# A list scheduler in the host code orders the recurrence, the weight preparation and the early blocks

## The chip, the cores and the metric

One core of a Trainium2 chip runs the whole program. The metric is device time in microseconds (us), the median of three runs. PE is the matrix engine, DVE, ACT and POOL are the vector, scalar and general-purpose engines, SP issues nearly all DMAs. Every engine executes its own list of instructions strictly in order; between engines there are semaphores. So the order in which the host code writes instructions is the order in which each engine runs them.

## The reference

A linear recurrence over 768 steps (32 heads of width 40) feeds two MLP layers over 3072 tokens.

```python
for t in range(S):
    y[:, :, t] = einsum('bhd,bhde->bhe', rt, state)
    Sa = einsum('bhde,bhe->bhd', state, at)
    state = state * wt[:, :, None, :] - outer(Sa, bt) + outer(vt, kt)
x = y.transpose(0, 2, 1, 3).reshape(3072, 320)
x = square(relu(x @ w_in)) @ w_out          # layer 0, d_ff 2048
h = x @ w_in2
out = (h * cos(h)) @ w_out2                 # layer 1
```

## The kernel before

**Recurrence.** The 768 steps are cut into 12 chunks of 64. For each chunk: DVE makes running products of the decay (`decay`, tiles lam and il in cin), the inputs are scaled (`compact_kb` on DVE, `compact_a` on POOL), PE forms a gram matrix (`gt`, PSUM tile pgt, masked by DVE into ga), which goes through DRAM (`gt_out`, `solve_load`, tile Ls) to a triangular solve of 28 small steps (`solve`, on POOL, for chunk 0 on DVE; tiles lent or l and ttmp), back through DRAM (`solve_store`, `load_t`, tiles Ts and tcomp) to `join`, four products that complete the inverse (pn, pn, pw, pt; the first is evicted by DVE as l<-pn). Then four independent groups of heads run `state`: products pq, px, pu, py and pm, each evicted by ACT or DVE before the next; pm gives the state that the next chunk needs. `pmat` (pp) prepares a part from the inputs alone. From chunk 3 on the tile l holds both the solve's matrix and a factor of `join`, so a solve cannot begin before the join of the chunk before it is through.

**Weights.** Those of both layers arrive as 64-bit words; ACT, DVE (u<-u, u<-w) and POOL turn them into f32, and ACT and POOL split them into a high and a low part (ws). The first 8 of 16 tiles of layer 0 are prepared in the opening, the others and half of layer 1 later.

**MLP.** Six blocks of 512 tokens per layer, 16 slices f each. In layer 0 a slice is 8 matmuls into a PSUM bank h, then Relu, Square and a rounded copy on ACT (g, gh), the rest gl on POOL, and 8 matmuls into po. Layer 1 has 8 and 12 (h, pt). A block needs two chunks of the recurrence; the last block of layer 0 and all of layer 1 come after the recurrence. PSUM has 8 banks: until the recurrence ends 3 for po, 1 for h and 4 that its products share (pool att); then h gets a second bank.

**Order.** `opening()` interleaves chunks 0 to 2 with weights by hand (`weave`); `period(c)` has a table of 42 time slots for each later chunk, and MLP units are paid out evenly over them, so that a block is nearly done when the next becomes ready. Operations of DVE pass through a helper, so they all carry line 151; they are told apart by their tiles.

Of the kernel before, what the change touches and what calls it, by code (L numbers as in the profile page):

```python
# [134 lines left out]
class Vector:  # L135

    def __init__(self, nc):
        self.real = nc.vector  # L140
        self.chain, self.credit = None, 0

    def link(self):
        if self.chain is not None and next(self.chain, 0) == 0:
            self.chain = None

    def __getattr__(self, name):
        fn = getattr(self.real, name)

        def call(*args, **kwargs):  # L150
            fn(*args, **kwargs)  # L151
            if self.credit > 0:
                self.credit -= 1
                self.link()

        return call

    def finish(self):
        while self.credit > 0 and self.chain is not None:
            self.credit -= 1  # L160
            self.link()
# [160 lines left out]
class Attn:  # L322
# [316 lines left out]
    def state(self, c, g):  # L639

        nc = self.nc
        ga, rv, mov = self.ga[c, g // 2], self.rv.pop((c, g)), self.mov.pop((c, g))
# [66 lines left out]
class Mlp:  # L709


    def __init__(self, tc, ctx, i, kc, xs, x2s, out, vec):
        self.vec = vec
        self.tc, self.nc, self.i, self.kc = tc, tc.nc, i, kc
        self.xs, self.x2s, self.out = xs, x2s, out
        self.p1 = ctx.enter_context(tc.tile_pool(name="m1", bufs=1))
        self.p2 = ctx.enter_context(tc.tile_pool(name="m2", bufs=2))
        self.po = ctx.enter_context(tc.tile_pool(name="mpo", bufs=1, space=PSUM))
        self.ph = ctx.enter_context(tc.tile_pool(name="mph", bufs=1, space=PSUM))
        self.ws, self.raw, self.xf, self.done = {}, {}, {}, set()  # L720
        self.xn = None
        self.ph2 = self.p3 = self.w2 = self.pending = None
        self.whole, self.more = set(), None
# [255 lines left out]
SOLVE, END = 8, 19  # L979

JOIN, GIN = (27, 30, 33, 36, 36), (37, 38, 40, 41)

TURN = 5


class Program:
    def __init__(self, tc, ctx, i, out, nch):
# [11 lines left out]
        self.vec = Vector(tc.nc)  # L999
# [49 lines left out]
    def run(self):  # L1049
# [6 lines left out]
        self.w1, self.w2 = self.W.first(EARLY), chain(self.W.rest(EARLY), self.W.second())  # L1056
        self.M.more = self.w2
# [5 lines left out]
        self.ctx1.close()  # L1063
        self.M.p3 = self.ctx2.enter_context(self.tc.tile_pool(name="m3", bufs=1))
# [8 lines left out]
    @staticmethod  # L1073
    def weave(*lists):

        todo = [((k + 0.5) / len(z), j, k, fn) for j, z in enumerate(lists) for k, fn in enumerate(z)]
        for _, _, _, fn in sorted(todo, key=lambda z: z[:3]):
            fn()

    def opening(self):  # L1080

        A, M = self.A, self.M
        self.gts = {c: A.gt(c) for c in range(4)}
        self.dcs = {c: A.decay(c) for c in range(1, 5)}
        cks = {c: A.compact_kb(c) for c in range(4)}
        join = {c: A.join(c) for c in range(4)}
        st = {c: [A.state(c, g) for g in range(4)] for c in range(3)}

        def s(gen, n=1):
            return [lambda: step(gen)] * n  # L1090

        def f(fn, *args):
            return [lambda: fn(*args)]

        def w(n):
            return s(self.w1, n)

        def prepare(c):
            out = s(self.dcs[c], 6)
            for q in range(4):  # L1100
                out += s(self.dcs[c], 2) + s(cks[c])
                if q % 2:
                    out += f(A.compact_a, c, q // 2)
            return out

        def gram(c):
            out = []
            for h in range(2):
                out += s(self.gts[c], 6) + f(A.gt_out, c, h, 0) + f(A.gt_out, c, h, 1)
            return out + f(A.solve_load, c)  # L1110

        def load(c):
            return f(A.load_w, c) + f(A.load_kb, c) + f(A.load_a, c)

        def solve(c, eng, n=4):
            z = A.solve
            box = []

            def go():
                if not box:  # L1120
                    box.append(A.solve(c, eng))
                step(box[0], n)

            return [go] * -(-30 // n) + f(A.solve_store, c) + f(A.load_t, c)

        def gin(c):
            return [lambda h=h, par=par: A.gt_in(c, h, par) for h in range(2) for par in range(2)] if c else []

        def fetch(c, g):
            return f(A.rv_load, c, g) + f(A.mov_load, c, g) + f(A.pmat, c, g)  # L1130

        def states(c, h):
            a, b = st[c][2 * h:2 * h + 2]
            out = []
            for k in range(5):
                out += s(a) + s(b)
            return out + f(A.y_store, c, h)

        for z in load(1):
            z()  # L1140
        A.zero()
        dc, g0 = A.decay(0), self.gts[0]
        for j in range(4):
            for _ in range(3):
                next(dc)
            next(cks[0])
            if j == 0:
                A.identities()
            A.compact_a(0, j, 4)
            if j == 2:  # L1150
                step(g0, 3)
        d1 = prepare(1)
        step(g0, 3)
        A.gt_out(0, 0, 0)
        A.gt_out(0, 0, 1)
        for z in d1[:3]:
            z()
        step(g0, 3)
        for z in d1[3:4]:
            z()  # L1160
        step(g0, 3)
        A.gt_out(0, 1, 0)
        A.gt_out(0, 1, 1)
        A.solve_load(0)
        step(self.w1, 5)
        for z in d1[4:9]:
            z()
        A.rv_load(0, 0)
        A.rv_load(0, 1)
        self.weave(solve(0, self.vec.real, 3), d1[9:] + load(2), w(5))  # L1170
        self.weave(gram(1), w(4), fetch(0, 0)[1:] + fetch(0, 1)[1:])
        A.keep_a(0)
        A.keep_a(1)
        pool = solve(1, A.nc.gpsimd, 2)
        self.weave(s(join[0], 5), s(self.dcs[2], 6))
        d2 = prepare(2)[6:]
        self.weave(states(0, 0), fetch(0, 2) + fetch(0, 3), w(6), pool[:8], d2[:3])
        self.weave(states(0, 1), fetch(1, 0) + fetch(1, 1), w(6), pool[8:], d2[3:])
        self.weave(s(join[1], 5) + gin(1), gram(2))
        A.keep_a(0)  # L1180
        A.keep_a(1)
        pool = solve(2, A.nc.gpsimd, 2)
        d3 = prepare(3)
        self.weave(states(1, 0), fetch(1, 2) + fetch(1, 3), w(8), pool[:8])
        self.weave(states(1, 1), fetch(2, 0) + fetch(2, 1), w(8), pool[8:], load(3))
        while next(self.w1, 0) is None:
            pass
        M.load_x(0, 0)
        self.weave(s(join[2], 5) + gin(2), s(self.w2, 10), d3[:6])
        self.ready = 0  # L1190
        self.weave(d3[6:] + s(self.gts[3], 9) + f(A.gt_out, 3, 0, 0) + f(A.gt_out, 3, 0, 1) + f(A.load_w, 4)
                   + s(self.dcs[4], 6), s(self.w2, 32), f(self.mlp, 1) * 40)

    def period(self, c):

        A, nch = self.A, self.nch
        more = c + 1 < nch
        st = [A.state(c, g) for g in range(4)]
        todo, rate = {}, {}

        def at(t, f, *args):
            todo.setdefault(t, []).append((f, args))

        for half in range(2):
            for t in ((15, 19, 23, 27, 31) if c < 2 else (20, 24, 28, 32, 36)) if half else (0, 4, 10, 14, 18):
                for q in range(2):
                    at(t, step, st[2 * half + q])
        at(2, A.rv_load, c, 2)
        at(6, A.rv_load, c, 3)
        at(6, A.mov_load, c, 2)  # L1210
        at(9, A.pmat, c, 2)
        at(14 if c < 2 else 16, A.mov_load, c, 3)
        at(14 if c < 2 else 19, A.pmat, c, 3)
        at(19, A.y_store, c, 0)
        at(33 if c < 2 else 37, A.y_store, c, 1)
        if more:
            for t in (0, 1, 2):
                at(t, step, self.gts[c + 1])
            if c:
                at(3, A.gt_out, c + 1, 1, 0)  # L1220
                at(3, A.gt_out, c + 1, 1, 1)
            if c:
                at(6, A.solve_load, c + 1)
# [148 lines left out]
```

## Time and profile before

| | |
|---|---|
| median of 3 runs | 1293.3 us (1292.32 to 1296.19) |
| the profiled execution | 1293.86 us, span 1292.1 us |
| mean granted TensorE clock | 0.923 of full speed |
| busy share PE / DVE / ACT / POOL | 86% / 55% / 56% / 43% |

The time of an execution is its span and 1.8 us around it. Busy shares are means over three stages that differ: an opening without MLP, a stretch in which recurrence and MLP share PE, and a tail of MLP alone. A matmul's record lasts longer than the time it takes from the next one, so PE's pace is read from starts, not from durations.

### The profile page before, as it was taken

How to read it: one execution, taken by the hardware profiler on the slowest of the kernel's cores; microseconds unless marked ns; L12 is line 12 of the kernel's file. 1: busy time of each engine (PE TensorE's matmuls, PEld its weight loads, DVE VectorE, ACT ScalarE, POOL GpSimd, SP SyncE). 2: the span in 40 equal slices, each digit the busy share in tenths (PEclk: the TensorE clock that was granted, in tenths of full speed). 3: DMA queues.
4: the chain of work that ended last, by engine and by line, in shares of the span. 5: the costliest groups of instructions: out<-in, count | busy, mean ns of one | idle time of the engine just before them, and what ended most of it. 6: DMA issues, size and time to landing. Idle time of an engine off the chain costs nothing.

```text
span 1292.1 us, 32595 instructions
## 1 busy us (share of the span) xinstructions
PE 1116.6 (86%) x13314; PEld 922.8 (71%) x13314; DVE 707.6 (55%) x1327; ACT 718.8 (56%) x1460; POOL 550.1 (43%) x788
## 2 busy tenths in 40 slices
PE   2467558796778989999999999998999999999997
PEld 2456446575556767777777777777889999999996
DVE  6774757667556556665656544124497343444432
ACT  2244555454374747574747475647756565655554
POOL 3261725626434251625252523125787333333332
PEclk9985758878779898999999999998999999999999
DMA  7532712535364343634363432126301010101000
GB/s 183 140 99 39 187 53 74 103 82 110 89 143 104 90 95 82 143 81 95 80 141 70 93 86 64 33 59 207 100 24 40 7 46 1 45 1 46 1 21 24
DMA packets 205147, 102.73 MB, mean 80 GB/s; under 512 B 163052, under 2 KB 185580, under 8 KB 204156
## 3 DMA queue, kind: packets, MB, share of 16 engines
q1 hardware_dynamic: 203154, 99.85, 31.7%
q8 instruction: 107, 1.75, 0.6%
q10 hardware_dynamic: 1834, 0.70, 0.2%
q14 instruction: 52, 0.43, 0.1%
HBM read 77.43 MB, written 23.09 MB: 78 GB/s over the span
## 4 chain that ended last, share of the span: by engine, by line
PE 58%; ACT 10%; POOL 10%; issue 7%; DMA 7%; DVE 5%; SPq 2%; ACTq 0%; POOLq 0%; DVEq 0%
PE h L941 23%; PE pt L883 13%; PE po L893 9%; PE pgt L479 3%; DMA w<-moe 2%; POOL ttmp L526 2%; PE pu L669 2%; POOL gl L792 2%; POOL u L188 2%; POOL l L529 1%; DVE u L151 1%; PE py L679 1%; PE pn L572 1%; PE pn L567 1%; POOL ws L220 1%
## 5 line engine op out<-in xcount | busy, mean ns | idle before, releaser
L941 PE MATMUL h<-xh,ws 128*128 128x512 f32 x960 | 334.1, 410 | 28.1 <-ACT g L789 19.6
L792 POOL TENSOR_TENSOR gl<-g,gh 128x512 fp32r<-128x512 f32 x96 | 129.7, 1352 | 300.0 <-ACT gh L791 197.7
L941 PEld LDWEIGHTS h<-xh,ws 128*128 128x128 f32 x960 | 183.1, 193 | 76.2 <-ACT g L789 28.0
L941 PE MATMUL h<-xl,ws 128*128 128x512 f32 x576 | 234.6, 407 | 0.1
L820 POOL TENSOR_TENSOR gl<-g,gh 128x512 fp32r<-128x512 f32 x96 | 125.3, 1305 | 190.8 <-ACT gh L819 158.8
L893 PE MATMUL po<-gh,ws 128*128 128x512 f32 x480 | 148.0, 427 | 3.5 <-ACT o L839 3.5
L789 ACT ACTIVATE g<-h 128x512 f32<-128x512 f32 x96 | 56.8, 592 | 148.7 <-PE h L941 143.7
L883 PE MATMUL pt<-ws,gh 128*128 128x320 f32 x768 | 128.1, 308 | 0.5 <-DVE g L151 0.4
L941 PEld LDWEIGHTS h<-xl,ws 128*128 128x128 f32 x576 | 110.9, 193 | 23.3 <-issue 2.6
L883 PEld LDWEIGHTS pt<-ws,gh 128*128 128x128 f32 x768 | 119.9, 188 | 8.3 <-DVE g L151 0.6
L800 ACT ACTIVATE n<-h 128x512 int32<-128x512 f32 x96 | 57.3, 596 | 119.9 <-PE h L941 119.9
L151 DVE SCALAR_TENSOR_TENSOR g<-n,h 128x512 f32<-128x512 int32 x96 | 66.0, 688 | 103.6 <-ACT n L800 100.8
L479 PE MATMUL pgt<-at,cin 40*128 40x104 f32 x768 | 73.4, 336 | 50.0 <-POOL at L455 41.6
L893 PEld LDWEIGHTS po<-gh,ws 128*128 128x128 f32 x480 | 93.9, 201 | 28.1 <-ACT o L839 3.9
L151 DVE TENSOR_TENSOR g<-g,h 128x512 f32<-128x512 f32 x96 | 65.8, 686 | 71.7 <-ACT g L804 71.7
L479 PEld LDWEIGHTS pgt<-at,cin 40*128 40x128 f32 x768 | 63.1, 236 | 57.3 <-POOL at L455 44.2
L188 POOL TENSOR_TENSOR u<-u,w 128x256 int32<-128x256 int32 (+2 forms) x80 | 57.0, 712 | 99.8 <-DVE u L151 80.5
L151 DVE TENSOR_TENSOR ga<-pgt,kc 128x416 f32<-128x416 f32 x96 | 52.8, 584 | 73.2 <-PE pgt L479 72.9
L893 PE MATMUL po<-gl,ws 128*128 128x512 f32 x288 | 90.2, 411 | 0.0
L151 DVE TENSOR_SCALAR u<-u 128x160 f32<-128x160 f32 (+9 forms) x160 | 61.5, 384 | 42.7 <-ACT u L176 39.7
L804 ACT ACTIVATE g<-g,kc 128x512 f32<-128x512 f32 x96 | 69.7, 726 | 26.5 <-DVE g L151 25.0
L151 DVE TENSOR_TENSOR mov<-pu,kc 64x416 f32<-64x416 f32 x96 | 56.5, 589 | 43.3 <-PE pu L670 30.4
(121 smaller groups left out, 2332.5 us busy)
## 6 DMA issues: line engine op xcount, KB each, us to landing
rv<-rv SPq DMA_DIRECT2D x48, 256.0 KB
w<-moe SPq DMA_DIRECT2D x16, 704.0 KB
cin<-cin SPq DMA_DIRECT2D x8, 832.0 KB
Ls<-ga SPq DMA_DIRECT2D x48, 128.0 KB
w<-moe SPq DMA_DIRECT2D x32, 160.0 KB
w<-moe SPq DMA_DIRECT2D x16, 256.0 KB
mov<-vt SPq DMA_DIRECT2D x96, 40.0 KB
xs<-yt SPq DMA_DIRECT2D x48, 80.0 KB
```

Of the source, the lines that this page charges most:

```text
L151: fn(*args, **kwargs)
L188: self.nc.gpsimd.tensor_tensor(t.bitcast(I32), u.bitcast(I32), w[:, :, 0], op=ALU.add)
L479: nc.tensor.matmul(pv[par][:, j], self.kb[r0:r0 + 40, p0 + j].rearrange("p h b -> p (h b)"), self.at[r0:r0 + 40, p0 + j], start=True, stop ...
L526: eng.tensor_tensor(tv, L[:, 0:j, j:j + 1].to_broadcast([128, j, n]), L[:, j:j + 1, j + 1:16].to_broadcast([128, j, n]), op=ALU.mult)
L789: nc.scalar.activation(g, h, AF.Relu)
L792: self.later.append((2, lambda: nc.gpsimd.tensor_tensor(gl, g, gh, op=ALU.subtract)))
L800: nc.scalar.activation(n, h, AF.Copy, bias=0.25, scale=float(np.float32(1.0 / (2.0 * np.pi))))
L804: nc.scalar.activation(g, g, AF.Sin, bias=self.kc[:, K_QT:K_QT + 1])
L820: nc.gpsimd.tensor_tensor(gl, g, gh, op=ALU.subtract)
L883: nc.tensor.matmul(self.pos[j][:, 0:DM], x[:, 128 * j:128 * j + 128], wo[:, DM * ws:DM * ws + DM], start=(f == 0 and x is gh and ws == 0), ...
L893: nc.tensor.matmul(self.pos[m], wo[:, 128 * ws:128 * ws + 128], x, start=(f == 0 and k in (0, 2, 4)), stop=(f == NF - 1 and k in (5, 6, 7)))
L941: nc.tensor.matmul(h, wi[:, ws], x[:, kt], start=(k == 0), stop=(k == 7))
```

## The change

The host code no longer writes instructions as it comes to them. A recorder (`Book`, `Engine`, `View`) takes each call, notes which tile regions it reads and writes, prices it (`price`) and keeps it. `run()` calls all tasks of recurrence (kind c), weights (w) and blocks 0 to 4 of layer 0 (m) in a plain order; `flush()` then simulates the five engines and the DMAs and emits one operation after another: always on the engine that can begin earliest, the candidate that can start first there (`slack` is 0), and among those that tie by `key`. On PE an MLP operation comes behind every recurrence operation, and two matmuls of the MLP stay together; elsewhere MLP operations come first. The rank is the longest priced path to the end. When the last recurrence operation is placed, what is left of weights and MLP follows in program order. The operations themselves, their number and their engines stay as they are. In PSUM, att goes from 4 banks to 3, and the freed bank becomes a second h (`ph3`), used by odd slices until the recurrence ends.

```diff
-        att = self.ctx1.enter_context(tc.tile_pool(name="att", bufs=4, space=PSUM))
+        att = self.ctx1.enter_context(tc.tile_pool(name="att", bufs=3, space=PSUM))
+        self.M.ph3 = self.ctx1.enter_context(tc.tile_pool(name="mph3", bufs=1, space=PSUM))
...
+        if self.ph2 is None and self.ph3 is not None and k % 2:
+            return self.ph3.tile([128, 512], F32, tag="h3", name="h")
...
-        self.opening()
-        for c in range(2, nch):
-            self.period(c)
-        all_of(self.w2)
...
+            book.kind = ("c", c)
+            do("join")
...
+                do("load", "decay", "kb", "a", "keep", "gram", "out", "tri", "solve", "inv")
...
+            for g in range(4):
+                for nm in ("rv", "mov", "pmat"):
+                    now[nm][g]()
+                do(f"state{g}")
...
+            if c % 2 and AHEAD <= c < nch - 1:
+                book.kind = ("m", c // 2)
+                self.ready = c // 2
+                n = UNITS if c == nch - 3 else 1000
+                while n and self.mlp(1):
+                    n -= 1
+        book.flush()
...
+        while need:
+            best = None
+            for e, c in cand.items():
...
+                    t = max(o.ready, r, free[e])
...
+                if fit and (best is None or t0 < best[0]):
+                    best = t0, e, fit
...
+            t, o = min(((t, o) for t, o in fit if t <= t0 + slack), key=lambda z: self.key(z[1], z[0] - t0, cfg))
...
+    def key(self, o, wait, cfg):
+        kind = o.kind[0]
+        if o.eng == "PE":
+            return (kind == "m", -o.rank + (o.cfg != cfg) * 500)
+        return (0 if kind == "m" else 1, -o.rank)
```

What this does to the lists is seen at three places. The first is DVE's list in the opening, ahead of the solve of chunk 0 (its steps read and write the tiles lent and ttmp). Before, the solve begins at row 33; lam_93 belongs to chunk 0 and lam_94 to chunk 1:

```order
25 L151 TENSOR_TENSOR ga<-pgt,kc 128x416 x2
26 L151 SCALAR_TENSOR_TENSOR lam_94<-lent,kc 104x259 x2
27 L151 SCALAR_TENSOR_TENSOR cin<-lent,kc 104x260
28 L151 RECIPROCAL lam_94<-cin 104x4
29 L151 TENSOR_TENSOR lam_94<-lam_94 104x4x63
30 L151 TENSOR_TENSOR cin<-lent,cin 104x512
31 L151 SCALAR_TENSOR_TENSOR cin<-lent,kc 104x260
32 L520 MEMSET lent 128x16
33 L526 TENSOR_TENSOR ttmp<-lent 128x14
```

Of the change (all recorded operations carry line 567), where lam_126 belongs to chunk 2 and the u tiles are weights; the solve begins only at row 54:

```order
16 L567 TENSOR_TENSOR mov<-pp,kc 64x4x64
17 L567 SCALAR_TENSOR_TENSOR cin<-lent,kc 104x260
18 L567 TENSOR_TENSOR mov<-pp,kc 64x4x64 x2
19 L567 SCALAR_TENSOR_TENSOR lam_126<-lent,kc 104x259 x4
20 L567 RECIPROCAL lam_126<-cin 104x4
21 L567 TENSOR_TENSOR mov<-pp,kc 64x4x64
22 L567 TENSOR_TENSOR lam_126<-lam_126 104x4x63
23 L567 TENSOR_TENSOR mov<-pp,kc 64x4x64 x2
24 L567 TENSOR_SCALAR u_235<-u_235 128x384
25 L567 TENSOR_SCALAR u_243<-u_243 128x384
```

The decay of chunks 1 and 2 and the first weights have moved ahead of the gram and the solve of chunk 0. The second place is SP's queue in the opening. Before, the gram of chunk 0 (Ls) leaves right behind the first inputs:

```order
5 L406 DMA lent<-cin 104x1024
6 L506 DMA Ts_135<-tt 128x528
7 L506 DMA Ts_136<-tt 128x528
8 L493 DMA Ls<-ga 64x8x64 x4
9 L514 DMA lent<-Ls 32x16x16 x4
10 L192 DMA w_236<-moe 128x1408
```

In the change inputs of `pmat` and `state` (rv, mov), two whole and one partial weight tile and inputs of chunk 2 stand ahead of it:

```order
7 L567 DMA rv<-rv 128x512 x2
8 L567 DMA mov<-vt 64x4x40 x6
9 L567 DMA w_198<-moe 128x1408
10 L567 DMA w_210<-moe 128x1408
11 L567 DMA rv<-rv 128x512
12 L567 DMA w<-moe 128x512
13 L567 DMA w<-moe 128x256
14 L567 DMA rv<-rv 128x512
15 L567 DMA lent<-cin 104x1040
16 L567 DMA rv<-rv 128x512
17 L567 DMA Ls<-ga 64x8x64 x2
```

What SP issues first has moved from the path of chunk 0 to loads for later. The third place is PE's list right behind the last product of the recurrence (py of chunk 11). Before, the accumulators po are those of block 4, whose last slices are under way:

```order
2920 L681 MATMUL py<-mov,ga 64x104
2921 L893 MATMUL po_10050<-gh,ws 128x512 x2
2922 L893 MATMUL po_10051<-gh,ws 128x512
2923 L893 MATMUL po_10051<-gl,ws 128x512
2924 L893 MATMUL po_10049<-gl,ws 128x512
2925 L893 MATMUL po_10050<-gl,ws 128x512
2926 L941 MATMUL h<-xh,ws 128x512
```

In the change po_8353 and po_8436 belong to block 2; blocks 3 and 4 follow whole:

```order
1550 L567 MATMUL py<-mov,ga 64x104
1551 L567 MATMUL h<-xh,ws 128x512
1552 L567 MATMUL h<-xl,ws 128x512
1553 L567 MATMUL po_8353<-gl,ws 128x512
1554 L567 MATMUL po_8436<-gl,ws 128x512
1555 L567 MATMUL po_8353<-gh,ws 128x512 x2
1556 L567 MATMUL po_8436<-gh,ws 128x512 x2
```

About two blocks of layer 0 have moved from between the chunks to behind the recurrence. Counted over PE's list, 616 matmuls into h and 594 into po stood ahead of the last py; now it is 382 and 330.

## Rows read from the trace of the kernel before

**Rows 1.** The page's part 1: engine, busy us, share of the span, instructions.
```profile
PE 1116.6 (86%) x13314; PEld 922.8 (71%) x13314; DVE 707.6 (55%) x1327; ACT 718.8 (56%) x1460; POOL 550.1 (43%) x788
```

**Rows 2.** Busy time by stretch: bounds, length, busy per engine, clock, DMA share, GB/s.
```profile
58.00:164.00 106.00, 67.76 (x1539) 59.59 (x1536) 65.08 (x128) 49.23 (x120) 55.42 (x109) 0.71 0.46 111
164.00:408.00 244.00, 186.28 (x2688) 143.24 (x2685) 156.11 (x322) 133.53 (x323) 111.13 (x199) 0.80 0.42 96
408.00:796.00 388.00, 361.12 (x5746) 281.84 (x5746) 222.22 (x450) 237.27 (x508) 154.10 (x271) 0.96 0.43 95
857.00:942.00 85.00, 81.50 (x346) 65.49 (x345) 35.26 (x48) 56.86 (x91) 48.33 (x39) 0.96 0.42 140
942.00:1285.00 343.00, 341.09 (x1900) 308.63 (x1898) 166.06 (x243) 192.72 (x324) 150.54 (x134) 1.00 0.07 22
```

**Rows 3.** Timeline of DVE: start us, us, instruction, [idle before it <-releaser].
```profile
58.08 0.69 DVE L151 TENSOR_TENSOR l<-pn,kc 128x512 f32<-128x512 f32 x1 [2.13 <-PE pn L567]
...
164.10 0.69 DVE L151 TENSOR_TENSOR l<-pn,kc 128x512 f32<-128x512 f32 x1 [2.14 <-PE pn L567]
...
408.10 0.69 DVE L151 TENSOR_TENSOR l<-pn,kc 128x512 f32<-128x512 f32 x1 [1.98 <-PE pn L567]
...
795.58 0.69 DVE L151 TENSOR_TENSOR l<-pn,kc 128x512 f32<-128x512 f32 x1 [1.52 <-DMA mov<-vt]
...
856.29 1.12 DVE L151 TENSOR_TENSOR yt<-sz,lam 104x256 f32<-104x256 f32 x1
```

**Rows 4.** Timeline of PE, 560 to 634 us.
```profile
562.51 1.09 PE L893 MATMUL po<-gh,ws 128*128 128x512 f32 x4
563.53 0.68 PE L617 MATMUL pp<-rv 40*64 40x64 f32 x16
564.15 0.50 PE L893 MATMUL po<-gh,ws 128*128 128x512 f32 x1
564.48 0.86 PE L893 MATMUL po<-gl,ws 128*128 128x512 f32 x3
...
568.00 0.25 PE L651 MATMUL pq<-rv,M0d 40*40 40x64 f32 x1
...
569.08 1.14 PE L479 MATMUL pgt<-at,cin 40*128 40x104 f32 x16
570.15 1.43 PE L893 MATMUL po<-gh,ws 128*128 128x512 f32 x5
...
585.72 0.28 PE L679 MATMUL py<-mov,ga 128*40 128x104 f32 x1
...
587.29 0.51 PE L941 MATMUL h<-xl,ws 128*128 128x512 f32 x1
...
604.17 1.29 PE L567 MATMUL pn<-t,ga 32*32 32x32 f32 x128
...
612.29 1.93 PE L572 MATMUL pn<-tcomp,l 32*32 32x32 f32 x128
...
619.53 1.20 PE L579 MATMUL pw<-t,ga 32*32 32x32 f32 x64
...
623.44 1.20 PE L586 MATMUL pt<-tcomp,l 32*32 32x32 f32 x64
```

**Rows 5.** The chain that ended last, at 952 us: start us, us, what.
```profile
952.36 1.84 PE h L941 x8
```

**Rows 6.** Groups of instructions of PE: busy us, mean ns, idle before them and releaser.
```profile
L941 PE MATMUL h<-xh,ws 128*128 128x512 f32 x960 | 334.1, 410 | 28.1 <-ACT g L789 19.6 <-ACT xh L756 8.3
```

**Rows 7.** Groups of instructions of DVE.
```profile
L151 DVE TENSOR_SCALAR u<-u 128x160 f32<-128x160 f32 (+9 forms) x160 | 61.5, 384 | 42.7 <-ACT u L176 39.7
L151 DVE TENSOR_TENSOR_SCAN cin<-cin,kc 104x260 f32<-104x260 f32 x36 | 33.7, 935 | 0.3
```

**Rows 8.** Tile lam: count, then ns min/median/max of one, first and last start.
```profile
L151 DVE TENSOR_TENSOR lam<-lam x48: 420/422/2765, 6.9 to 711.0; 104x252 f32<-104x252 f32 x48
```

**Rows 9.** Timeline of POOL at 580 us.
```profile
580.18 0.13 POOL L520 MEMSET l<- 128x16 f32 x1
```

More of the change, by code (lines that the diff above doesn't have):

```diff
@@ L1 @@
-from contextlib import ExitStack
+from contextlib import ExitStack, contextmanager
 from itertools import chain
@@ L132 @@
 LOW_WORD, HIGH_WORD = f32_of_bits(0x38100000), f32_of_bits(0x47EFFFFF)
[L135 to L145, printed above, removed]
-    def __getattr__(self, name):
[L148 to L161, printed above, removed]
+ENGINES = {"tensor": "PE", "scalar": "ACT", "vector": "DVE", "gpsimd": "POOL", "sync": "SP"}
@@ new lines, with groups @@
+FIRST = {"ACT": 33, "DVE": 34, "POOL": 95, "SP": 27, "PE": 54}
+SPARED = {"ACT": 95, "DVE": 80, "POOL": 40, "SP": 0, "PE": 0}
+OUTSTANDING = 8
+def groups(side):
+    out, inner = [], None
+    for t in side.replace("(", " ( ").replace(")", " ) ").split():
+        if t == "(":
+            inner = []
+        elif t == ")":
+            out.append(inner)
+            inner = None
+        elif inner is None:
+            out.append([t])
+        else:
+            inner.append(t)
+    return out
@@ new lines, with __init__, __getattr__, call @@
+class Op:
+    __slots__ = ("k", "eng", "fn", "args", "kw", "outs", "ins", "kind", "preds", "succs", "spots", "cfg", "cost", "full",
+                 "left", "ready", "start", "end", "rank", "calls", "dma", "seen")
+class Engine:
+    def __init__(self, book, nc, name):
+        self.book, self.real, self.name = book, getattr(nc, name), name
+    def __getattr__(self, method):
+        fn = getattr(self.real, method)
+        def call(*args, **kw):
+            if self.book.direct:
+                return fn(*[real(z) for z in args], **{k: real(z) for k, z in kw.items()})
+            self.book.note(ENGINES[self.name], method, fn, args, kw)
+        return call
@@ L975, in step @@
             break
[L979 to L983 removed]
+UNITS = 1000
 class Program:
@@ L1071, in run @@
         General(self).run()
[L1073 to L1192, printed above, removed]
@@ new lines, in tasks, with each, steps, call @@
+    def tasks(self, c):
+        A, nch = self.A, self.nch
+        out = {}
+        def each(name, *fns):
+            out[name] = list(fns)
+        def steps(name, gen, n):
+            out[name] = [lambda: step(gen)] * n
+        def call(fn, *args):
+            return lambda: fn(*args)
+        if c:
+            each("load", call(A.load_w, c), call(A.load_kb, c), call(A.load_a, c))
+        else:
+            each("ident", A.identities)
+        steps("decay", A.decay(c), 14 if c else 12)
+        steps("kb", A.compact_kb(c), 4)
+        n = 4 if c == 0 else 8
+        each("a", *(call(A.compact_a, c, h, n) for h in range(NP // n)))
+        steps("gram", A.gt(c), 12)
+        halves = [(h, par) for h in range(2) for par in range(2)]
+        each("out", *(call(A.gt_out, c, *z) for z in halves))
+        if c:
+            each("keep", call(A.keep_a, 0), call(A.keep_a, 1))
+            each("in", *(call(A.gt_in, c, *z) for z in halves))
+        each("tri", call(A.solve_load, c))
+        steps("solve", A.solve(c, A.nc.vector if c == 0 else A.nc.gpsimd), 29)
+        each("inv", call(A.solve_store, c), call(A.load_t, c))
+        steps("join", A.join(c), 5)
+        for nm, fn in (("rv", A.rv_load), ("mov", A.mov_load), ("pmat", A.pmat)):
+            each(nm, *(call(fn, c, g) for g in range(4)))
+        for g in range(4):
+            steps(f"state{g}", A.state(c, g), 5 if c < nch - 1 else 4)
+        each("y", call(A.y_store, c, 0), call(A.y_store, c, 1))
+        return out
@@ L1294, in run @@
         tc, nc = g.tc, g.tc.nc
+        for nm in ("xs", "x2s", "w2f", "kc", "bad"):
+            setattr(g, nm, real(getattr(g, nm)))
         flag = nc.values_load(g.bad.bitcast(I32), skip_runtime_bounds_check_because="only compared with zero")
```

456 lines of the change are left out of this document (366 added, 90 removed).

## Prediction

> **What bounds the kernel now.** I read the busy shares first: PE 86% [rows 1], nothing else over 56%. That is a mean, so next the busy time by stretch [rows 2], cut at marks that the timeline gives: the first, third, sixth and twelfth time that DVE evicts the first join product (58, 164, 408 and 796 us) and the last output of the recurrence at 856.3 + 1.1, 857 us [rows 3]. From 942 to 1285 PE is busy 341 of 343 us at full clock: the tail is PE at its pace, and no order makes it shorter. From 58 to 408 PE is busy 254 of 350 us at a granted clock of 0.71 and 0.80, a mean between its two levels (1.2 GHz reads as 0.5, 2.4 GHz as 1). The time to win lies there.
>
> To see how much, I price PE's work at full clock from the starts in its timeline [rows 4]. Four po matmuls from 562.51 to 563.53 are 4 x 0.23 us and 0.10 for going over to another kind of product; the po at 564.15 takes 0.33 to the next start, 0.10 more again. The chain in the tail has 1.84 us for eight h, 0.23 each [rows 5]. So: 0.23 us for an MLP matmul of layer 0, 0.10 for each change of kind. For one chunk of recurrence: pgt four times 1.07 (569.08 to 570.15), pp four times 0.62, pq twice 1.08 (568.00 to 569.08), py twice 1.57 (585.72 to 587.29), px and pu like py as they have the same 104 columns, pm as pq scaled from 64 to 40 columns (1.4), and the join rows less the 0.07 by which a row runs over the next start: 1.22 + 1.86 + 1.13 + 1.13. That is 4.3 + 2.5 + 2.2 + 9.4 + 1.4 + 5.3, about 25 us a chunk, 297 in all (chunk 0 has no pq, the last no pm).
>
> Between the sixth and the twelfth join six chunks take 387.5 us, 64.6 each [rows 3]; PE's work per chunk there is 25.1 + 128 MLP matmuls x 0.23 = 29.4 + 38 changes x 0.10 = 58.3, which is 90%. From the third join to the end of the recurrence it is 240 + 1210 x 0.23 + 363 x 0.10 = 554 us of work in 693: 80%. The stretch from 164 to 408 alone has 155 in 244: 64%. Ahead of the third join there are 57 us of work in 164.
>
> **The change, part by part.** No instruction is added or removed, so the sum is PE's work plus what PE loses, stage by stage.
>
> The opening. PE waits there; DVE is the engine to count. Each operation in DVE's list at the mean of its group (two of them in [rows 7]) gives the work ahead of the first, second and third eviction l<-pn: 52, 85 and 120 us before, 82, 107 and 158 in the change. Of the 30 us at the first, 20 more u operations at 0.384 and 9 of their second kind at 0.46 make 12, eight more backward scans at about 0.93 make 7.5, the rest is four forward scans and smaller work. All of it stands ahead of the solve of chunk 0, and the gram's stores stand behind weight loads on SP, so the path of chunk 0 itself gets longer: now DVE's 52 us took 58 [rows 3], and 82 should take 88. At the third join DVE's list was idle for 44 of 164 us, waiting for the chain. The change fills that idle: 158 us of work. Bounds: 160 with no gap, 202 with all of the old 44; I take 170, near the first, because the list is now long enough to cover most of the waits. The order that gives up 30 us at the first chunk has got back all but 6 at the third, and weights that were converted after 164 lie ahead of it.
>
> Third join to the end of the recurrence. Less MLP stands in it: 712 matmuls instead of 1210. PE's work is 238 + 712 x 0.23 = 164 + 436 changes x 0.10 = 44, together 446 us. Nothing else needs more: DVE's operations there sum to 533 - 158 = 375 us, ACT's and POOL's to fewer. The longest loop from chunk to chunk is the one through tile l: in the trace a solve starts on POOL at 580.18 [rows 9] and the last join product is through at 624.6 [rows 4], 44 us with MLP work between its steps, and some 4 for the next load, 48 a chunk. The nine periods from the third to the twelfth join are 432 us of it: PE is still the longest, but not by much. At what share of PE? Bounds: 64% of the worst stretch, 99% of the tail. I take the 90% of the steady stretch, since mixed work of this kind was held there for 388 us, and the second h bank removes a wait that the 90% contains: PE's h is idle 28.1 us in all, 19.6 of them for ACT to read the one bank [rows 6]; that is at most 2% of the stretch, and the three att banks instead of four may take it back. 446 / 0.90 = 496 us, so the recurrence ends at 170 + 496 = 666 instead of 857.
>
> The tail. 498 matmuls x 0.23 = 114.5 us have moved into it: 435 us from 857 to the end of the span become 549.5. Before, 85 us from 857 to 942 held 326 x 0.23 = 75 us of work [rows 2]: 10 lost at the change of stage, waiting for inputs of block 5. These now have blocks 3 and 4 to hide behind; I take back 5 of the 10 (bounds 0 and 10). If POOL and ACT could not hold PE's pace the cover would go, but in those 85 us they were busy 48 and 57, late weights included.
>
> Sum: 666 + 549.5 - 5 = 1210.5 of span, 1212 with the 1.8 us around it. The profiled execution (1293.86) lies 0.6 above the median, so no correction.
>
> A rule against trust in the 90%: the Trainium skill, Perfetto Trace Analysis, section Identifying the Most-Contended Engine, holds that matmul busy time is no measure of nearness to the roofline and that the busy share of weight loads is. By weight loads the steady stretch has 282 of 388 us (73%), the tail 309 of 343 (90%) [rows 2], which would make it 81% of the tail's density and not 90; by that share over the whole stretch the time would be 1267. The trace agrees on PE's busy record, which shows 361 of 388 us where starts give 350; but recurrence products load small weights, so I stay with starts.
>
> **Rivals.**
> *The recurrence keeps its losses (chance 0.20).* PE's share from the third join on stays at the 80% of now, because the waits are those of the chain, the weights and a low clock, and the order only shifts MLP into the tail. 446 / 0.80 = 558, end at 728, time 1274. For it: the clock of 0.80 up to 408 came with gaps that weights caused, and the change has as many weights. Against it: 60 instead of 32 of the first u operations lie ahead of the third join.
> *Slower: a fixed order stalls every engine in line (0.14).* An operation placed by a planned landing time is late, and all behind it on its engine wait, as POOL's solve steps behind a gl that waits for ACT, with PE's next product behind them. It decides at 1298: the recurrence would have to end at 751, 581 us after the third join, 77% of PE. At the 64% seen from 164 to 408 the end would be 867 and the time 1413; at 74% 1319. For it: that stretch exists, and SP's queue holds gram stores behind loads. Against it: the same in-order queues gave 90% for 388 us.
> *DVE and POOL hold each other up (0.06).* A lam product on DVE takes 420 to 2765 ns [rows 8], so something does stop it. If none of the about 100 us that POOL's list holds ahead of the third join could run beside DVE's operations with two SBUF inputs, two thirds of its work, the third join came 67 us later less the 12 of gap that I allow: 1267. The Trainium skill, Trainium Architecture — The Big Picture, section What this means for kernel authors, calls the port that DVE and GpSimd share an exclusive lock. The trace agrees only in part: from 58 to 164 DVE's 65 and POOL's 55 us sum to 120 in 106 [rows 2], so they do overlap, and the group means that I used hold these delays already.
> *Better (0.15).* The order reaches 97% from the third join on and that comes at 165: end at 625, time 1170; PE cannot do more than the 1285 - 942 = 343 of the tail at 99%.
> *The change does nothing measurable (0.05).* Shorter chunks and a longer tail cancel: an end between 743 and 751 is within 0.3%, about what a measurement of this kernel can tell.
>
> **How the numbers follow.** My forecast, 88 to 93% from the third join on and that join at 160 to 180, has the remaining 0.40 and spans 1190 to 1235; its middle is 1212. Cases faster by over 0.3%: 0.40 + 0.20 + 0.06 + 0.15, same 0.05, slower 0.14. Below the range I leave a third of the better case and above it most of the slower one: 1160 to 1305.
>
> **What would show it.** In the changed kernel's profile: first l<-pn at about 88 us and third near 170; first h close behind; six chunks late in the recurrence at about 52 us each instead of 64.6; last yt near 666 with PE's clock near 1 from 200 us on; then some 190 us of h and po at full pace before the first pt. It would be wrong if the third join lies past 200, if PE shows waits of several us for ACT or DVE once in each chunk, or if the tail shows idle PE.

## The result and the profile after

The changed kernel takes 1233.55 us (median of 4 runs, 1229.23 to 1237.48), the kernel before in the same comparison 1294.34: a ratio of 0.953, 95% interval 0.9494 to 0.9566. The forecast was 1212 in a range of 1160 to 1305. The profiled execution is the fastest of the four: 1229.23 us, span 1227.2.

Busy shares first, the page's part 1 of the changed kernel (engine, busy us, share, instructions); beside [rows 1] PE went from 86% to 89%:

```profile
PE 1097.7 (89%) x13314; PEld 910.6 (74%) x13314; DVE 668.8 (54%) x1327; ACT 713.0 (58%) x1460; POOL 541.7 (44%) x788
```

The marks, from DVE's timeline of the changed kernel, answer to [rows 3]: the first, third, sixth and twelfth eviction of the first join product and the last output of the recurrence.

```profile
91.20 0.68 DVE L567 TENSOR_TENSOR l<-pn,kc 128x512 f32<-128x512 f32 x1
...
176.57 0.66 DVE L567 TENSOR_TENSOR l<-pn,kc 128x512 f32<-128x512 f32 x1
...
345.27 0.69 DVE L567 TENSOR_TENSOR l<-pn,kc 128x512 f32<-128x512 f32 x1
...
648.81 0.69 DVE L567 TENSOR_TENSOR l<-pn,kc 128x512 f32<-128x512 f32 x1 [3.23 <-PE pn L567]
...
679.44 0.42 DVE L567 TENSOR_TENSOR yt<-sz,lam 104x256 f32<-104x256 f32 x1
```

The opening is 12.5 us longer (164.1 to 176.6). From the third join to the last yt it was 693.3 us and is 503.3. What follows was 434.7 and is 547.3. So 12.5 - 190.0 + 112.6 = -64.9 us of span. The next view shows busy time by stretch of the changed kernel (columns as in [rows 2]):

```profile
91.00:177.00 86.00, 67.45 (x1500) 60.18 (x1502) 62.78 (x150) 51.25 (x130) 51.86 (x102) 0.76 0.43 100
...
177.00:345.00 168.00, 155.12 (x2808) 119.74 (x2806) 115.18 (x255) 105.12 (x250) 75.97 (x149) 0.92 0.51 116
345.00:649.00 304.00, 283.63 (x5382) 217.73 (x5384) 197.63 (x442) 193.66 (x451) 124.35 (x257) 0.94 0.51 117
...
680.00:880.00 200.00, 196.70 (x859) 160.46 (x858) 44.39 (x56) 123.38 (x200) 92.99 (x75) 0.99 0.22 73
880.00:1220.00 340.00, 338.51 (x1886) 306.44 (x1884) 163.92 (x239) 190.25 (x320) 148.40 (x131) 1.00 0.06 21
```

Three chunks from the third to the sixth join took 244 us at a clock of 0.80 and take 168 at 0.92; most of what PE no longer loses lies here (69 of 80 us, worked out at the end). Blocks 3 and 4 at the head of the tail run like the rest of it (196.7 of 200 us). The group that answers to [rows 6], of the changed kernel, stands as two lines, since the MLP of the tail is written directly:

```profile
L299 PE MATMUL h<-xh,ws 128*128 128x512 f32 x560 | 183.9, 393 | 2.3 <-ACT g L299 2.3
...
L567 PE MATMUL h<-xh,ws 128*128 128x512 f32 x400 | 146.7, 426 | 1.7 <-ACT g L567 1.6
```

The 28.1 us that PE's h was idle are down to 4.0. What else PE waits for between 177 and 680 us is small too (what was waited for, us in total, times, longest):

```profile
PE pn L567 <- issue: 5.9, 7, 1.3
PE pq L567 <- issue: 5.1, 1, 5.1
PE pp L567 <- issue: 3.0, 2, 1.6
PE pm L567 <- DVE MT L567: 2.1, 1, 2.1
```

**One account for all runs.** PE's work from the third join to the last yt is priced as in the prediction: the recurrence that is left (236 to 240 us), n MLP matmuls ahead of the last py at 0.23, changes of kind at 0.10. "Lost" is the time between the two marks less this work. "Tail by sum" is 547.3 + (712 - n) x 0.23, the changed kernel's tail for another n. Marks are of the profiled execution, medians of all runs, ratios against runs of the kernel before beside them; names that end in no_w are runs without the late weight conversions.

| kernel | median us | ratio (95%) | n | third join, last yt | work | lost | tail, by sum |
|---|---|---|---|---|---|---|---|
| before | 1293.3 | 1 | 1210 | 164.1, 857.4 | 555 | 138 | 435, 433 |
| change | 1233.55 | 0.953 (0.9494 to 0.9566) | 712 | 176.6, 679.9 | 445 | 58 | 547, 547 |
| hand_no_w | 1261.25 | 0.9743 (0.9711 to 0.9775) | 1210 | 166.9, 827.1 | 555 | 106 | 436, 433 |
| sched_no_w | 1234.57 | 0.9534 (0.9486 to 0.9583) | 712 | 172.0, 689.0 | 444 | 73 | 548, 547 |
| hand_two_h | 1345.65 | 1.0421 (1.0374 to 1.0467) | 1210 | 170.0, 904.8 | 555 | 180 | 436, 433 |
| one_h | 1263.59 | 0.9755 (0.9719 to 0.9791) | 580 | 164.3, 668.5 | 407 | 97 | 600, 578 |
| hand_drip | 1368.45 | 1.0576 (1.0537 to 1.0614) | 712 | 163.8, 807.4 | 439 | 204 | 549, 547 |
| hold_w | 1243.21 | 0.9621 (0.9569 to 0.9672) | 784 | 179.9, 709.2 | 457 | 72 | 532, 531 |
| by_rank | 1233.35 | 0.9533 (0.9494 to 0.9573) | 1078 | 175.0, 765.7 | 530 | 61 | 466, 463 |
| dma0 | 1293.9 | 1.0008 (0.9983 to 1.0032) | 644 | 181.7, 728.5 | 428 | 118 | 564, 563 |
| dma2 | 1238.45 | 0.9575 (0.9526 to 0.9625) | 866 | 178.3, 723.3 | 478 | 67 | 513, 512 |
| hop | 1234.2 | 0.9535 (0.9458 to 0.9613) | 828 | 173.7, 711.5 | 473 | 65 | 521, 521 |
| flat | 1269.59 | 0.9813 (0.9755 to 0.9871) | 794 | 183.7, 737.0 | 463 | 90 | 531, 528 |
| one_h_no_w | 1217.12 | 0.9397 (0.937 to 0.9424) | 698 | 169.4, 661.8 | 435 | 57 | 551, 551 |

The tail is what the sum says within some 3 us in all but one, one_h. So the kernels differ mainly in what PE loses between the two marks (and by up to 20 us in when the third join comes), and the change took that from 138 to 58 us; by the sum, the MLP that moved is worth nothing either way.

### The profile page after: what moved, and what is told of

Read it like the earlier page. It is cut to its first block, busy times and chain, and to the rows that moved or that the text cites. A ratio compares the mean times of both kernels' runs of the same rounds, so it can differ in the third digit from the quotient of the medians.

```text
span 1227.2 us, 32639 instructions
## 1 busy us (share of the span) xinstructions
PE 1097.7 (89%) x13314; PEld 910.6 (74%) x13314; DVE 668.8 (54%) x1327; ACT 713.0 (58%) x1460; POOL 541.7 (44%) x788
## 4 chain that ended last, share of the span: by engine, by line
PE 71%; DVE 9%; ACT 7%; DMA 6%; issue 5%; POOL 1%; SPq 1%; ACTq 0%; DVEq 0%; POOLq 0%
PE h L299 16%; PE pt L299 13%; PE h L567 11%; PE po L567 10%; PE pgt L567 3%; PE px L567 3%; PE pn L567 3%; PE po L299 2%; PE py L567 2%; PE pu L567 2%; DVE mov L567 2%; DVE u L567 2%; PE pp L567 2%; PE pq L567 1%; DMA cin<-cin 1%
## 5 line engine op out<-in xcount | busy, mean ns | idle before, releaser
L299 POOL TENSOR_TENSOR gl<-g,gh 128x512 fp32r<-128x512 f32 x113 | 147.8, 1308 | 218.6 <-ACT gh L299 176.4
L299 PE MATMUL h<-xh,ws 128*128 128x512 f32 x560 | 183.9, 393 | 2.3 <-ACT g L299 2.3
L567 POOL TENSOR_TENSOR gl<-g,gh 128x512 fp32r<-128x512 f32 x79 | 104.0, 1326 | 183.0 <-ACT gh L567 142.3
L567 PE MATMUL h<-xh,ws 128*128 128x512 f32 x400 | 146.7, 426 | 1.7 <-ACT g L567 1.6
L299 PE MATMUL h<-xl,ws 128*128 128x512 f32 x336 | 132.5, 394 | 0.1
L567 POOL TENSOR_TENSOR u<-u,w 128x160 int32<-128x160 int32 (+4 forms) x80 | 55.7, 702 | 151.4 <-DVE u L567 132.9
L567 PE MATMUL po<-gh,ws 128*128 128x512 f32 x385 | 118.4, 412 | 1.3 <-ACT o L567 0.8
L567 PE MATMUL h<-xl,ws 128*128 128x512 f32 x240 | 98.8, 412 | 0.0
L567 PEld LDWEIGHTS po<-gh,ws 128*128 128x128 f32 x385 | 69.9, 190 | 19.6 <-ACT o L567 1.5
L567 ACT ACTIVATE g<-h 128x512 f32<-128x512 f32 x79 | 46.4, 594 | 56.9 <-PE h L567 52.1
L567 PE MATMUL po<-gl,ws 128*128 128x512 f32 x231 | 75.7, 409 | 0.7 <-POOL gl L567 0.7
```

What stands on the lines that cost most here:

```text
L299: return fn(*[real(z) for z in args], **{k: real(z) for k, z in kw.items()})
L567: fn(*[real(z) for z in args], **{k: real(z) for k, z in kw.items()})
```

## The experiments

**Late weights.** `hand_no_w` (of the kernel before) and `sched_no_w` (of the change) take the late conversions out:

```diff
-                self.nc.sync.dma_start(st["u"], self.i[nm][f, :, c0:c0 + n])
+                self.nc.sync.dma_start(st["u"], self.i["rv"][0, 0].rearrange("p a b -> p (a b)")[:, 0:n])
...
-            if not self.raw:
+            if True:
...
-        return self.pieces("moe2", range(LATE if self.raw else 0), 5, ...
+        return self.pieces("moe2", (), 5, ...
```

> The hand order, with the conversion of the weights of layer 0 from tile 8 on and of half of layer 1 left out (their values are taken from another input, so the output is not the reference's; splits and matmuls stay). Theory S: the hand order loses its time between the third and the sixth join (244 us for 155 us of PE's work) because the conversions of late weights stand in line on SP, ACT, DVE and POOL and make each other wait. Then that stretch falls to about 175 us and the time to about 1225. Rival P: the slots of the hand table are too long for the chain and the scheduler gains by moving MLP into the tail. Then the stretch stays above 220 us and the time above 1270.

> The scheduled order with the same conversions left out (the output is not the reference's). Theory S: the scheduler has already taken the stalls of the weights away, so little is left: a time of 1195 to 1225, 10 to 40 us below the scheduled kernel, most of it ahead of the third join, where DVE's list gets 19 us shorter. Rival P: the gain of leaving out is as large as in the hand order or larger, 60 us, a time near 1170.

Measured: 1261.25, between the two readings, and 1234.57, above both. In the hand order the late weights cost 32 us, of which 23 lie between the third and the sixth join (221 us instead of 244; 175 was expected if they were the cause of all that is lost there). Under the scheduler with its two h banks they cost nothing that can be measured (with one h bank it is otherwise, as shown below). So they explain at most 32 of the 80 us less that are lost, and the other reasons for the hand order's losses stayed when they were gone.

**The bank alone.** `hand_two_h` is the hand order with three att banks and two for h:

```diff
-        att = self.ctx1.enter_context(tc.tile_pool(name="att", bufs=4, space=PSUM))
+        att = self.ctx1.enter_context(tc.tile_pool(name="att", bufs=3, space=PSUM))
+        self.M.ph3 = self.ctx1.enter_context(tc.tile_pool(name="mph3", bufs=1, space=PSUM))
```

> The hand order with three att banks and a second h bank, nothing else. Theory S: the second bank takes away at most the 19.6 us in which PE's h waits for ACT, and three att banks may cost as much: 1272 to 1296. Rival B: the bank is what the change gains by: 1250 or less.

> The scheduler with four att banks and one h bank. PE's list then has 580 instead of 712 MLP matmuls ahead of the end of the recurrence, so the tail is 30 us longer. Theory S: the share of PE from the third join on falls by a few points with the waits for the one bank, 407 us of work at 85%: end near 655, time 1225 to 1250. Rival B: without the bank most of the gain is lost: 1270 or more.

Measured: 1345.65, slower by 4.2% and outside both readings. PE's waits from 164 to 880 us, of this kernel, and its last output of the recurrence:

```profile
PE pgt L479 <- ACT sz L656: 21.0, 9, 3.8
PE pgt L479 <- POOL at L455: 18.7, 8, 5.1
PE pn L567 <- DVE t L151: 11.2, 6, 7.3
```

```profile
903.71 1.12 DVE L151 TENSOR_TENSOR yt<-sz,lam 104x256 f32<-104x256 f32 x1
```

The wait of h for ACT's read (19.6 us before) is gone from this list. In its place pgt, the product that opens a chunk, waits 21.0 us for ACT to copy pq into sz; pgt does not read sz, but it shares the att banks with pq, and that wait does not stand among those of the kernel before. DVE feels it behind: its ga waits for pgt 97.1 us in this stretch, 64.0 before. Between the marks PE loses 180 us instead of 138; the tail is as long as before (436 against 435). The waits named do not add up to the 42 us more. The granted clock is lower too (0.76 from the third to the sixth join and 0.92 to the twelfth; [rows 2] has 0.80 and 0.96), which, counted as for dma0 below, is worth at most 0.24 x 250 + 0.08 x 423 = 94 us against 64, so 30 of the 42. The rest is not accounted for.

`one_h`, the other half, is the scheduler with four att banks and one h (the lines of the diff above the other way round). Measured: 1263.59, between the two readings. By itself this would say: 30 us by the scheduler, 30 by the bank. The trace shows something else in it. This is where PE stood longest, just behind the recurrence, with POOL's timeline of the same moment:

```profile
690.49 1.65 PE L567 MATMUL po<-gl,ws 128*128 128x512 f32 x3 [17.36 <-POOL gl L567]
```

```profile
676.23 0.62 POOL L567 TENSOR_TENSOR u<-u,w 128x160 int32<-128x160 int32 x1 [5.29 <-DVE u L567]
...
682.04 0.77 POOL L567 TENSOR_TENSOR u<-u,w 128x256 int32<-128x256 int32 x1 [4.27 <-DVE u L567]
...
687.21 0.53 POOL L567 TENSOR_TENSOR u<-u,w 128x160 int32<-128x160 int32 x1 [3.58 <-DVE u L567]
688.69 0.53 POOL L567 TENSOR_TENSOR u<-u,w 128x160 int32<-128x160 int32 x1 [0.96 <-ACT g L567]
689.17 3.73 POOL L567 TENSOR_TENSOR gl<-g,gh 128x512 fp32r<-128x512 f32 x3
```

When the last operation of the recurrence is placed, the rest follows in program order; here weights were left over, each comes from its load, and the gl that PE needs stands behind them on POOL. That is 22 us of this kernel's tail (600 by the marks, 578 by the sum), 17.4 of them in this one piece, and PE waits there for no PSUM bank. So a further run took the late weights out of it too.

> The scheduler with four att banks and one h bank, and with the late weight conversions left out (their loads come from rv, so the output is not the reference's); 698 MLP matmuls ahead of the last py, where the run with two h banks and no late weights has 712. In the run with one h bank and all weights PE waited 17.4 us in one piece at 690 us, behind the last recurrence operation: POOL's gl stood behind u operations of weights that were left over and came one after another from their loads. Theory 'most of what one h bank cost is this stall': without the weights the stall is gone, time 1235 to 1250, 0 to 15 us above the two-bank run (1234.6). Rival 'the second h bank is worth 30 us by itself, in the recurrence': 1258 or more.

Measured: 1217.12 (interval of the ratio 0.937 to 0.9424), better than expected by either reading, and 17 us faster than the same with two h banks (0.9486 to 0.9583). Without the late weights, then, the second bank is no gain at all; with them, it is 30 us. What these runs do show is the order by itself: with the same banks the scheduler is 30 us faster than the hand order with the late weights (one_h and the kernel before; 97 against 138 us lost) and 44 us faster without them (one_h_no_w and hand_no_w; 57 against 106). Beyond the stall the weights cost the scheduler with one h bank 40 us of lost time (97 against 57). How a bank decides what becomes of the weights is not settled: I saw where the 22 us went, not the 40. One of the two runs compared here, sched_no_w, has a single period of 74.5 us (481.9 to 556.3; the others behind the third join are 45 to 60). Most of its length is work, with 122 MLP matmuls in it; by the account 15 us of it are lost, against 3 in the same period of one_h_no_w. So some 12 of the 17 us may be one bad place in one plan.

**Less MLP between the chunks.** `hand_drip` keeps the hand order and pays out as much MLP as the change does (it also no longer loads a block's input ahead of its turn; PE's one wait for such an input, xh, is 8.3 us as before):

```diff
+PAY = 0.78
...
-            self.acc = min(self.acc + max(self.left, 12) / to, 3)
+            self.acc = min(self.acc + PAY, 3)
```

> The kernel before with its order written by hand and its four att banks, but layer 0 of the MLP is paid out at 0.78 of a unit per slot, so that 712 of its matmuls stand ahead of the last py, as many as in the change (before: 1210); the tail then has the 549.5 us of the prediction's sum. Rival 'less MLP between the chunks is the gain' : the recurrence keeps its share of 80% of PE or better, 444 us of work in 555 us or less, end at 720 or earlier, time 1265 or less. Theory 'the order of the chunks is the gain': the steps of a chunk stay as far apart as the slots put them, PE idles where MLP work was, the periods stay above 60 us, end past 745, time 1290 or more.

Measured: 1368.45, slower by 5.8%. In the hand order MLP was the filling between the steps of a chunk. With 498 matmuls fewer the recurrence became only 50 us shorter (its work 116), and PE's waits from 389 to 761 us show the steps themselves:

```profile
PE pn L567 <- DVE t L151: 22.3, 6, 5.9
PE pgt L479 <- ACT M0d L705: 15.0, 5, 3.7
PE pq L651 <- ACT M0d L705: 9.0, 2, 8.8
```

The granted clock in this window is 0.86; from 408 to 796 before it was 0.96. So moving MLP into the tail is not the gain; it takes an order in which the chunks come closer together when MLP is taken out.

**The place of MLP.** `by_rank` is the change without the rule that MLP comes last on PE:

```diff
-            return (kind == "m", -o.rank + (o.cfg != cfg) * 500)
+            return -o.rank + (o.cfg != cfg) * 500
```

> The scheduler without the rule that an MLP matmul comes behind every recurrence product on PE; 1078 instead of 712 MLP matmuls then stand ahead of the last py. Theory 'PE's work is conserved, its place does not matter as long as PE is kept busy': the last yt comes about 366 x 0.23 / 0.89 = 95 us later, near 775, the tail is shorter by 84, time 1228 to 1246. Rival 'moving MLP to the tail is itself worth time, because mixed stretches run at 89% and the tail at 99%': the moved 84 us cost 10 us or more in the mixed stretch, time 1246 or more.

Measured: 1233.35, the same as the change. 366 MLP matmuls more stand ahead of the last py, the last yt comes 85.8 us later (366 x 0.23 = 84), and the tail is 81 us shorter. Its joins up to the ninth lie within 3 us of the change's and the twelfth 5.5 us later: about 320 of the 366 stand behind the twelfth join, among the last products of the recurrence. PE loses 61 us between the marks instead of 58. So the run shows that MLP may as well stand ahead of the last products as behind them; of more MLP between the chunks it says little.

**The opening.** `hold_w` lets no weight operation be placed until the solve of chunk 0 is:

```diff
+                    if o.kind[0] == "w" and not all(done[p] for p in hold):
+                        continue
```

> The scheduler with one rule more: no weight operation is placed until the solve of chunk 0 is placed whole, so the path of chunk 0 loses the u operations and weight loads ahead of it. Theory 'the sum of DVE's work sets the third join': the first join comes earlier (about 75 instead of 91 us), the third not before 168, time 1222 to 1240. Rival 'the longer path of chunk 0 is what the opening costs': the third join comes at 155 or earlier, as much earlier as the first, time 1215 or less.

Measured: 1243.21, 3 us above the upper end of the theory. The first join comes 8 us earlier than in the change and the third 3 us later (DVE's timeline of this kernel):

```profile
83.43 0.69 DVE L570 TENSOR_TENSOR l<-pn,kc 128x512 f32<-128x512 f32 x1 [0.37 <-PE pn L570]
...
179.87 0.69 DVE L570 TENSOR_TENSOR l<-pn,kc 128x512 f32<-128x512 f32 x1 [0.61 <-PE pn L570]
```

So an earlier chunk 0 is not enough for an earlier third join. That DVE has to do ahead of the third join what it puts off would be a reason, but it is only argued: DVE is idle for some 40 of these 180 us too. Most of the 10 us that this run is slower arise behind that join (72 us lost against 58).

**The prices of the plan.** Four runs give the scheduler other prices. `dma0` takes the fixed times of a DMA out, `dma2` doubles them:

```diff
-                st = t + o.cost + 1350
+                st = t + o.cost
...
-                o.end = land + 350
+                o.end = land
```

`hop` adds 100 ns to each handover between engines (`FIRST`), and `flat` prices all of DVE, ACT and POOL alike:

```diff
+        if eng != "PE" and dma is None:
+            cost = 500.0
```

> The scheduler with a wrong plan: the fixed times of a DMA (1350 ns ahead of a transfer and 350 ns behind it) are priced at nothing, so its lists assume that gram, solve and inverse come back from DRAM 1.7 us earlier each; the rest is as in the change, with 644 MLP matmuls ahead of the last py instead of 712. Theory 'the gain is the kind of order, most urgent first, MLP in the gaps, and not the exact times': 1225 to 1250. Rival 'a fixed order is only as good as its prices, what is planned too early stalls all behind it': 1270 or more.

> The scheduler with the fixed times of a DMA priced at twice those of the change (2700 and 700 ns instead of 1350 and 350); 866 MLP matmuls instead of 712 stand ahead of the last py, which is 35 us of work moved out of the tail and no gain by itself. Theory 'lead time: what arrives earlier than planned costs nothing, what arrives later stalls a list': PE waits for DMA as little as in the change or less (rv 10 us or less), time 1210 to 1236. Rival 'an order is as good as its prices are right, an error to either side costs': lists wait for work that was placed too late, time 1260 or more.

> The scheduler with 100 ns more in the plan for each handover from one operation to the next engine's (FIRST: 133, 134, 195, 127 and 154 ns instead of 33, 34, 95, 27 and 54); 828 MLP matmuls ahead of the last py. The plan of the change ends the recurrence at 569 us and the trace at 680, 1.19 times as late from the first join on; with the hop priced higher the plan itself is longer by 7%. Theory 'lead time': as with the doubled DMA times, 1210 to 1236. Rival 'errors to either side cost': 1250 or more.

> The scheduler with every operation of DVE, ACT and POOL priced at 500 ns, whatever its shape (their rows go from 0.2 to 1.4 us); matmuls and DMAs are priced as in the change; 794 MLP matmuls ahead of the last py. Theory 'lead time of the DMAs is the price that matters': 1225 to 1250. Rival 'every price matters, the engines' as much as the DMAs': 1270 or more.

Measured: 1293.9, 1238.45, 1234.2 and 1269.59. With DMAs priced 1.7 us shorter than in the change the scheduler gains nothing: 0.9983 to 1.0032 of the time before. I had expected that the kind of order would carry the gain without exact times (1250 at most), and that failed. The two stretches of dma0 from its third to its sixth and twelfth join, PE's wait for rv in it from 170 to 700 us, and ACT's for weights:

```profile
182.00:358.00 176.00, 159.79 (x2717) 122.44 (x2712) 106.70 (x235) 99.47 (x233) 71.36 (x143) 0.86 0.45 99
358.00:689.00 331.00, 282.65 (x5346) 221.84 (x5346) 199.16 (x453) 187.53 (x439) 114.67 (x254) 0.87 0.49 109
```

```profile
PE pp L567 <- DMA rv<-rv: 20.8, 7, 6.0
...
ACT w L567 <- DMA w<-moe: 48.9, 19, 8.0
```

In the change ACT's wait for these loads is 10.3 us in the same window, and PE's for rv is not among those of 0.7 us or more. The plan has each load land 1.7 us early and places what uses it accordingly; what lands later than planned holds the whole list of the engine that needs it. PE's named waits add up to less than the 60 us more that are lost: the granted clock is 0.86 and 0.87 where the change has 0.92 and 0.94. If every hundredth of clock is a hundredth of the stretch, that is 0.14 x 176 + 0.13 x 331 = 68 us, in the change 0.08 x 168 + 0.06 x 304 = 32, so at most 36 of the 60 come by way of the clock.

A price too long costs little: with DMA times doubled it is 5 us, with 100 ns more for each handover 1, and the intervals of both overlap with the change's. dma2 missed the upper end that I gave it by 2 us; its mechanism held, as no wait of PE for a DMA stands out in it. `flat` loses 36 us, which falls at the rival's 1270: prices of the engines matter too, though a plan that knows nothing of them is still better than the order by hand.

## Why the prediction was right, point by point

**The opening.** Forecast 88 us for the first join and 170 for the third; measured 91.2 and 176.6, inside the bounds of 160 to 202. The reason held less well than the number. I had added up DVE's work at the means of its groups, 158 us, and allowed 12 of gap. But successive records of DVE overlap, and the busy time up to the third join, of the kernel before, the change and one_h (columns as in [rows 2]), shows a list with more gaps:

```profile
0.00:164.00 164.00, 87.39 (x1824) 77.38 (x1824) 108.90 (x229) 65.19 (x152) 74.64 (x139) 0.81 0.53 128
...
0.00:177.00 177.00, 94.04 (x1836) 83.36 (x1838) 133.20 (x305) 81.03 (x200) 95.96 (x172) 0.88 0.55 138
...
0.00:164.00 164.00, 96.77 (x1888) 86.06 (x1888) 132.78 (x297) 79.52 (x195) 89.43 (x163) 0.84 0.60 149
```

In the change DVE is idle for 44 of 177 us, in the kernel before it was for 55 of 164: the gap was not filled as forecast. The work was put 25 us too high and the gap 32 too low, and that 170 came so near is in part luck. Nor does DVE's work alone set this time, for one_h has as much of it ahead of its third join and reaches that join 12 us earlier, the first 19 us earlier:

```profile
71.75 0.69 DVE L567 TENSOR_TENSOR l<-pn,kc 128x512 f32<-128x512 f32 x1 [0.53 <-PE pn L567]
...
164.26 0.68 DVE L567 TENSOR_TENSOR l<-pn,kc 128x512 f32<-128x512 f32 x1
```

one_h has the fourth att bank and another plan with it; which of the two brings the join forward, no run shows.

**PE's share from the third join on.** Forecast 90%, 446 us of work in 496; measured 445 in 503.3, which is 88.4%. Six late chunks take (648.81 - 345.27) / 6 = 50.6 us each, forecast about 52. The account by starts is tested by the tails, which it gives within some 3 us in all but one_h; lost time is what it leaves over, so between the marks it can't fail.

**The tail.** Forecast 544.5 us, measured 547.3. I had taken back 5 of the 10 us lost at its head; by the sum it was 549.5 - 547.3 = 2.2. From 680 to 880 us PE is busy for 196.7 of 200.

**The sum.** 170 + 496 + 544.5 = 1210.5 forecast, 176.6 + 503.3 + 547.3 = 1227.2 measured. The error of 16.7 is 6.6 of opening, 7.3 of share and 2.8 of tail. The median lies 4.3 above the profiled execution.

**Where a reason was wrong.** The step on the second h bank ("at most 2% of the stretch, and the three att banks instead of four may take it back") treated it as a small term of its own. It has no size of its own: +52 us in the hand order, -30 under the scheduler, +17 under the scheduler without late weights. The 19.6 us of idle time in [rows 6] did vanish, and said nothing about what the att bank was worth.

I also had PE's clock near 1 from 200 us on; it is 0.92 and 0.94 up to the twelfth join.

**The rivals.** That the recurrence keeps its losses was wrong for the change (88% instead of 80%) and its form in hand_drip is far from paying. The stall of a fixed order was given 0.14; it did not come, but dma0 shows it whole: 547 us between the marks for 428 of work, 78%, and no gain. What stands between the forecast and that case is 1.7 us in the price of a DMA. I had seen the mechanism and had no row from which to read how near it was. DVE and POOL did not shut each other out: from 91 to 177 us they are busy 62.8 + 51.9 = 114.7 us in 86. Whether they slow each other, no run here was made to show.

The rule of the Trainium skill (Perfetto Trace Analysis, section Identifying the Most-Contended Engine) to go by the busy share of weight loads, which it names together with the share of the peak rate (MFU), gave 1267. The trace does not bear it out here: weight loads fill 72% of 345 to 649 and 90% of the tail, 80% of its density, where the work by starts is 272 of 304 us, 89%.

**Where the gain came from.** The time between the marks fell by 190.0: 110 of work (114.5 of MLP moved into the tail and 2 of recurrence ahead of the third join, 73 more changes of kind took back 7) and 80 us less lost. Of these, (244 - 155) - (168 - 148) = 69 lie between the third and the sixth join, where the clock rose from 0.80 to 0.92: 0.20 x 244 - 0.08 x 168 = 35 at most by way of the clock. Late weights in the hand order are worth 32 of the 80, shown by hand_no_w. That the order is a cause by itself is shown by the two pairs with equal banks (30 us with the late weights, 44 without). How it saves PE's time, no run here took apart further: hand_drip and, for the last chunk, by_rank show what it is not, dma0 and flat that it hangs on the plan's times.

## What to carry to other kernels

Price PE's work by starts, take the length of each stretch less that work, and look for the cause of the difference; in by_rank and the tails by sum, which stretch MLP stood in was worth nothing as long as PE found work. Price a static order's loads and handovers long rather than short: here 1.7 us too little for a load took the whole gain, and twice the price cost 5 us. And try a buffer's worth only under the order with which it will run: here the same bank was 52 us of loss, 30 of gain and 17 of loss.

## What the runs showed of the hardware that I had not expected

PE's granted clock falls in the mixed stretch of the changed kernel although PE's waits there are short. Four windows of 10 us of it (length, PE busy, clock, DMA share, GB/s):

```profile
477.00:487.00 10.00, 9.62 (x172) 1.00 0.58 132
487.00:497.00 10.00, 7.87 (x84) 1.00 0.34 55
497.00:507.00 10.00, 8.08 (x284) 0.50 0.23 67
507.00:517.00 10.00, 10.00 (x175) 0.99 0.23 52
```

From 497 to 507 us it stood at 0.50, the lower of its two levels (1.2 GHz), the whole time. Ahead of it PE was busy 7.9 of 10 us, with a wait of 2.1 us for DVE up to 495.3; in it, behind one more wait of 1.9 us, it ran 284 matmuls, more than in the others, since those of the recurrence are small; in the next 10 us it was back at 2.4 GHz. Ten us at the lower level are at most 5 us of PE's time, as much as PE's longest wait in this stretch (5.1).
